# Turning the memory rows in two column parts and interleaving the Q and K passes by part in a recurrent attention layer

## The chip, the cores and the metric

The kernel runs on one core of one Trainium2 chip. The metric is the time of one launch on the device in microseconds (us). PE is the tensor engine, PEld its weight loads, DVE the vector engine, ACT the scalar engine, POOL (Pool) the general engine.

## The reference, cut to what matters

Four layers run on 2048 tokens of width 640: A, B, A, B. Only B is touched. It walks through 64 segments of 32 tokens, and each segment's first 8 rows are the memory that the segment before produced, so the steps cannot overlap freely:

```python
mem = mem0                                             # 8 memory rows
for s in range(n_seg):                                 # 64 steps, 32 tokens each
    h = jnp.concatenate([mem, xs], axis=1)             # 40 rows
    q, k, v = (einsum('btd,dhe->bhte', h, W) for W in (Wq, Wk, Wv))
    p = softmax(where(mask, einsum('bhqe,bhke->bhqk', q, k) * scale, -1e9))
    o = einsum('bhqk,bhke->bhqe', p, v)
    o = einsum('bhte,hed->btd', o, Wo)
    mem = o[:, :M, :]                                  # what the next step waits for
    outs.append(o[:, M:, :])
```

With two layers B there are 128 steps and 126 boundaries between steps.

## The kernel before

The width of 640 is held as NCH = 5 chunks of 128. `hT[s]` is the transposed input of step s; its columns 24:32 of each chunk are the memory rows. A pass (Q or K for one half of the heads) is five parts, one for each chunk, of four matmuls each. When a pass is complete, DVE transposes its result (`turn`) and casts the memory columns into `QT` or `KT`, which the scores read.

```python
def part(c):                                           # 4 matmuls, one for each column group of PE
    for j in range(4):
        nc.tensor.matmul(ps[32*j:32*j+32, :], lhsT=cols(c), rhs=wsel(Wt, c, b, j),
                         start=(c == 0), stop=(c == NCH-1), tile_position=(0, 32*j), ...)

class QKPass:
    def run(self, k=NCH):
        while k > 0 and self.parts:
            self.parts.pop(0)(); k -= 1
        if not self.parts:
            tq = turn(self.ps[:])                                         # DVE transpose, b_TQ
            place("dve", tq, self.b, heads(self.dst[s]), 0, 8, 24)        # DVE cast, memory columns
            if not last:
                place("pool", tq, self.b, heads(self.dst[s + 1]), 8, 32, 0)
# ... one step:
qk(W.wq, "b_Qa", 0, QT)
qk(W.wk, "b_Ka", 0, KT)
qk(W.wq, "b_Qb", 1, QT)
K1 = QKPass(W.wk, "b_Kb", 1, KT)
K1.run(2)
scores(0)             # mask matmuls, then matmuls whose weights are KT: first reader of b_KT
K1.run(3)
# ...
if i4 == 0 and T + 1 < NT:
    tail_cols(T + 1)  # Pool: the tail rows' copy b_hx, used a step later
V0 = VPass(0); V0.run(1); sums(0); normalise(0); V0.run(4)
# ... scores(1), V1, values(0), sums(1), normalise(1), values(1), filler pieces in between ...
op.run(8)             # last part of the output projection b_OPS
TM = wk.tile([128, 10, 32], F32, name="b_TM", tag="TM")
nc.vector.transpose(out=TM[:].rearrange("p g t -> p (g t)"), in_=ops[:])
for hf in range(2):
    nc.vector.tensor_tensor(out=hT[s + 1][64*hf:64*hf+64, :, 24:32], in0=TM[0:64, hf:10:2, 24:32],
                            in1=TM[64:128, hf:10:2, 24:32], op=ALU.add)
fill(9)               # the rest of the filler: tail passes (b_tail) or a deferred projection (b_OPSd)
```

The filler is work that no step waits for, put where PE would be idle. Steps come in fours (i4 = 0 to 3). Step 0 has b_OPSd as filler, steps 1, 2 and 3 have the V, Q and K passes of the next tile's tail rows (b_tail; called V, Q and K tails below). PSUM is the memory that PE writes its results to; the results of the passes, the scores and the fillers rotate through three slots.

## Time and profile before

| | before |
|---|---|
| median of the first 3 runs | 2334.03 us (2330.82 to 2334.85) |
| span of the profiled run | 2335.8 us |
| a step of layer B | 12.9 to 13.5 us |

The page of the profile, its busy times and the first line of its chain of what ended last:

```profile
PE 2225.5 (95%) x54988; PEld 1238.1 (53%) x54988; DVE 1576.3 (67%) x3618; ACT 950.3 (41%) x2207; POOL 1036.7 (44%) x2475
...
PE 80%; DVE 10%; ACT 5%; issue 2%; DMA 2%; POOL 0%; SPq 0%; DVEq 0%; ACTq 0%; POOLq 0%
```

PE is the bound, and DVE is 10% of the chain. The groups by form (busy us, mean ns of one, then idle time before them) give the costs of the operations in question:

```profile
L85 DVE STREAM_TRANSPOSE b_TM<-b_OPS 128x320 f32<-128x320 f32 x126 | 65.1, 517 | 118.2 <-PE b_OPS L85 118.2
...
L85 DVE TENSOR_TENSOR b_hT<-b_TM 64x40 bf16<-64x40 f32 x252 | 56.1, 223 | 8.6
```

The table of waits (total us, times, longest us):

```profile
PEld L85 <- DVE b_hT L85: 66.6, 126, 1.7
...
PEld L85 <- DVE b_KT L85: 16.0, 100, 0.2
```

A timeline of one step boundary, behind Q tails and into a step with i4 = 3. The columns are start us, duration us, engine, line, operation, output<-inputs, shapes, count, and in brackets the idle time before it with its releaser:

```profile
781.95 1.25 PE L85 MATMUL b_tail<-b_wq,b_hx 128*32 128x512 bf16 x20
...
782.18 0.52 DVE L85 STREAM_TRANSPOSE b_TM<-b_OPS 128x320 f32<-128x320 f32 x1 [0.44 <-PE b_OPS L85]
...
782.73 0.54 DVE L85 TENSOR_TENSOR b_hT<-b_TM 64x40 bf16<-64x40 f32 x2
...
783.32 3.36 PEld L85 LDWEIGHTS <-b_hT 128*32 128x32 bf16 x68 [0.61 <-DVE b_hT L85]
783.32 1.26 PE L85 MATMUL b_Qa<-b_wq,b_hT 128*32 128x512 bf16 x20
...
784.71 0.72 DVE L85 STREAM_TRANSPOSE b_TQ<-b_Qa 128x512 f32<-128x512 f32 x1 [0.69 <-POOL b_QTt L85]
785.46 0.23 DVE L85 CAST b_QT<-b_TQ 128x128 bf16<-128x128 f32 x1
...
785.79 0.72 DVE L85 STREAM_TRANSPOSE b_TQ<-b_Ka 128x512 f32<-128x512 f32 x1
786.54 0.23 DVE L85 CAST b_KT<-b_TQ 128x128 bf16<-128x128 f32 x1
...
787.00 0.24 PE L85 MATMUL b_SP<-c_mask,c_identb 128*32 128x160 bf16 x4
787.00 0.11 PEld L85 LDWEIGHTS <-b_KT 128*32 128x32 bf16 x4
...
787.30 0.41 PE L85 MATMUL b_Kb<-b_wk,b_hT 128*32 128x512 bf16 x4
```

The 20 filler matmuls start at 781.95. Matmuls of this form follow each other 54 ns apart when nothing is in the way (b_Qa to b_Ka in the same step: 20 in 1.09 us), so the filler covers 1.08 us and ends its issue at 783.03. DVE needs until 783.27 for the memory rows, and b_Qa starts at 783.32: PE lost 0.29 us. I call the start of b_Qa less the end of the filler's issue the boundary gap, and read it at all 126 boundaries. Its mean is 0.28 us behind K tails, 0.18 behind V tails, 0.29 behind Q tails, 0.04 behind b_OPSd (30 boundaries each), 1.28 at four boundaries without filler, and about 1.3 at each layer's first.

The lower half of the extract is the path that the change puts at risk: b_KT is finished 3.45 us after the start of b_Qa (786.77 - 783.32), and its first reader is a weight load at 3.68 us.

### The profile page before, as it was taken

Reading aid. Unit: us, or ns where it says so; the run is one execution under the profiler, and the core shown is the slowest. Engines: PE = TensorE matmul, PEld = TensorE weight load, DVE = VectorE, ACT = ScalarE, POOL = GpSimd, SP = SyncE. Lnnn points to the kernel's source line nnn. Section 1 sums busy time; section 2 is a strip of 40 time slices with the busy share of each in tenths; the row PEclk is TensorE's granted clock in tenths of the full one; section 3 lists DMA queues with packets and bytes.
Section 4 is the critical chain, followed back from the end, with each engine's and each line's share of the span. In section 5 each row is a group of like instructions: output and inputs, shape, how many; then the busy total and the mean of one; then the engine's idle time right before and its main releaser. Section 6 shows DMA issues by size and latency. Waiting matters only on the chain.

```text
span 2335.8 us, 122651 instructions
## 1 busy us (share of the span) xinstructions
PE 2225.5 (95%) x54988; PEld 1238.1 (53%) x54988; DVE 1576.3 (67%) x3618; ACT 950.3 (41%) x2207; POOL 1036.7 (44%) x2475
## 2 busy tenths in 40 slices
PE   6999989999999999999889899899999999999997
PEld 3444545555555555555545445455555555555554
DVE  5777746666666666666657777566666666666664
ACT  5776823323232333323257767223333233323332
POOL 3344534444444444444324445344444444444442
PEclk9999989999999999999989999999999999999998
DMA  6555540000000000000133334300000000000000
GB/s 165 146 148 152 161 142 20 21 18 20 18 19 19 20 21 20 21 15 17 31 104 115 108 117 127 124 18 15 17 15 17 16 18 16 17 18 16 14 12 14
DMA packets 90649, 123.38 MB, mean 53 GB/s; under 512 B 16496, under 2 KB 80000, under 8 KB 88192
## 3 DMA queue, kind: packets, MB, share of 16 engines
q1 hardware_dynamic: 87648, 111.84, 16.9%
q8 instruction: 431, 7.06, 1.3%
q10 hardware_dynamic: 2464, 3.61, 0.6%
q14 instruction: 106, 0.87, 0.1%
HBM read 89.17 MB, written 26.21 MB: 49 GB/s over the span
## 4 chain that ended last, share of the span: by engine, by line
PE 80%; DVE 10%; ACT 5%; issue 2%; DMA 2%; POOL 0%; SPq 0%; DVEq 0%; ACTq 0%; POOLq 0%
PE b_OPS L85 14%; PE b_V L85 13%; PE b_Qa L85 7%; PE b_tail L85 7%; PE b_Kb L85 6%; PE b_Ka L85 6%; PE b_Qb L85 6%; PE b_SP L85 4%; PE a_PP L85 4%; ACT a_PT L85 4%; PE b_OTL L85 3%; PE b_OPSd L85 3%; PE a_S L85 2%; PE a_pv L85 2%; DVE a_qk L85 2%
## 5 line engine op out<-in xcount | busy, mean ns | idle before, releaser
L85 PEld LDWEIGHTS <-b_hT 128*32 128x32 bf16 x15120 | 369.8, 96 | 334.7 <-DVE b_hT L85 66.6
L85 ACT ACTIVATE b_PT<-b_SP 128x224 bf16<-128x224 f32 x256 | 92.2, 360 | 784.6 <-DVE b_TQ L85 740.2
L85 PE MATMUL b_V<-b_wv,b_hT 128*32 128x512 bf16 x5040 | 355.8, 381 | 0.0
L85 ACT ACTIVATE a_PT<-a_S 128x768 bf16<-128x768 f32 (+1 forms) x384 | 326.7, 892 | 62.4 <-PE a_S L85 56.2
L85 PE MATMUL b_OPS<-b_wo,b_OTsb 128*32 128x320 bf16 x8192 | 329.9, 303 | 6.5 <-DVE b_OTsb L85 5.2
L85 PEld LDWEIGHTS <-b_OTsb 128*32 128x32 bf16 x8192 | 197.3, 97 | 115.4 <-DVE b_OTsb L85 49.4
L85 POOL CAST b_QT<-b_TQ 128x384 bf16<-128x384 f32 x254 | 142.7, 562 | 240.9 <-DVE b_TQ L85 240.9
L85 ACT CAST b_OTsb<-b_OTL 128x320 bf16<-128x320 f32 x384 | 151.0, 428 | 232.3 <-PE b_OTL L85 204.7
L85 POOL CAST b_KT<-b_TQ 128x384 bf16<-128x384 f32 x254 | 142.9, 563 | 175.5 <-DVE b_TQ L85 174.3
L85 POOL TENSOR_TENSOR b_PT<-b_PT,b_R 128x64 bf16<-128x64 bf16 x256 | 105.6, 412 | 222.1 <-ACT b_R L85 197.4
L85 POOL TENSOR_SCALAR_AFFINE_SELECT a_PT<-a_PT 128x256 bf16<-128x256 bf16 x256 | 109.0, 427 | 172.6 <-ACT a_PT L85 161.0
L85 PE MATMUL b_Kb<-b_wk,b_hT 128*32 128x512 bf16 x2520 | 182.5, 380 | 0.0
L85 PE MATMUL b_Qa<-b_wq,b_hT 128*32 128x512 bf16 x2520 | 162.3, 387 | 13.7 <-DVE b_hT L85 7.2
L85 PE MATMUL b_Ka<-b_wk,b_hT 128*32 128x512 bf16 x2520 | 160.0, 383 | 0.0
L85 PE MATMUL b_Qb<-b_wq,b_hT 128*32 128x512 bf16 x2520 | 158.1, 380 | 0.0
L85 PE MATMUL a_PP<-a_xnT,a_wt 128*128 128x512 bf16 x560 | 146.1, 394 | 5.2 <-DVE a_um L85 1.5
L85 DVE STREAM_TRANSPOSE b_TM<-b_OPS 128x320 f32<-128x320 f32 x126 | 65.1, 517 | 118.2 <-PE b_OPS L85 118.2
L85 PE MATMUL a_S<-a_qk 32*128 32x512 bf16 (+3 forms) x1024 | 137.3, 308 | 7.8 <-ACT a_PT L85 6.5
L85 DVE CAST b_Vsb<-b_V 128x512 bf16<-128x512 f32 x128 | 88.5, 692 | 74.6 <-PE b_SP L85 43.9
L85 DVE TENSOR_TENSOR b_PT<-b_PT,b_R 128x160 bf16<-128x160 bf16 x256 | 103.8, 405 | 48.3 <-ACT b_R L85 29.2
L85 DVE STREAM_TRANSPOSE b_TQ<-b_Qa 128x512 f32<-128x512 f32 x128 | 91.7, 717 | 65.7 <-PE b_Qa L85 45.4
L85 DVE CAST b_OTsb<-b_OTL 128x320 bf16<-128x320 f32 x128 | 62.9, 492 | 106.0 <-PE b_OTL L85 105.2
(165 smaller groups left out, 4270.0 us busy)
## 6 DMA issues: line engine op xcount, KB each, us to landing
a_wt<-a_wpad SPq DMA_DIRECT2D x112, 160.0 KB
b_XO<-xres SPq DMA_DIRECT2D x256, 30.0 KB
a_wvo<-in_A_wo_dram SPq DMA_DIRECT2D x8, 800.0 KB
b_wq<-in_B_Wq_dram SPq DMA_DIRECT2D x20, 256.0 KB
b_wk<-in_B_Wk_dram SPq DMA_DIRECT2D x20, 256.0 KB
xres<-a_xo SPq DMA_DIRECT2D x16, 320.0 KB
xres_bf<-a_xb SPq DMA_DIRECT2D x32, 160.0 KB
b_wv<-in_B_Wv_dram SPq DMA_DIRECT2D x20, 256.0 KB
```

Of the source, the lines that this page charges most:

```text
L85: r = f(*a, **k)
```

## The change

The intent is to let PE begin the next step on chunks 0 and 1 while DVE still turns the other three, and to have enough matmuls on those two chunks (Q and K, 16 of them) to bridge the rest. The tail rows' copy on Pool moves from before the first scaling to behind the second. The whole diff:

```diff
-            qk(W.wq, "b_Qa", 0, QT)
-            qk(W.wk, "b_Ka", 0, KT)
+            Q0, K0 = QKPass(W.wq, "b_Qa", 0, QT), QKPass(W.wk, "b_Ka", 0, KT)
+            Q0.run(2)
+            K0.run(2)
+            Q0.run(3)
+            K0.run(3)
             qk(W.wq, "b_Qb", 1, QT)
@@
             while xn_pending:
                 ln_tr(xn_pending.pop(0))
-            if i4 == 0 and T + 1 < NT:
-                tail_cols(T + 1)
             V0 = VPass(0)
@@
             normalise(1)
+            if i4 == 0 and T + 1 < NT:
+                tail_cols(T + 1)
             if g_need < NT:
@@
                 TM = wk.tile([128, 10, 32], F32, name="b_TM", tag="TM")
-                nc.vector.transpose(out=TM[:].rearrange("p g t -> p (g t)"), in_=ops[:])
-                for hf in range(2):
-                    nc.vector.tensor_tensor(out=hT[s + 1][64 * hf:64 * hf + 64, :, 24:32], in0=TM[0:64, hf:10:2, 24:32],
-                                            in1=TM[64:128, hf:10:2, 24:32], op=ALU.add)
+                for c0, c1 in ((0, 2), (2, NCH)):
+                    nc.vector.transpose(out=TM[:, 2 * c0:2 * c1].rearrange("p g t -> p (g t)"), in_=ops[:, 64 * c0:64 * c1])
+                    for hf in range(2):
+                        nc.vector.tensor_tensor(out=hT[s + 1][64 * hf:64 * hf + 64, c0:c1, 24:32], in0=TM[0:64, 2 * c0 + hf:2 * c1:2, 24:32],
+                                                in1=TM[64:128, 2 * c0 + hf:2 * c1:2, 24:32], op=ALU.add)
```

## The prediction

> **What bounds the kernel.** PE is busy 95% of the span and holds 80% of the chain that ended last (the page). Layer B is 128 recurrent steps of about 13.0 us. At each boundary (timelines of PE) the last 32 b_OPS matmuls are covered by 20 tail matmuls (54 ns apart, 1.08 us) or 36 b_OPSd matmuls (1.22 us). Meanwhile DVE runs one 128x320 transpose (517 ns) and two 64x40 adds (about 200 ns each, 310 to 370 ns where Pool's b_OTdef copy overlaps); b_Qa needs all of it, 1.16 us after b_OPS. By b_Qa's start less the filler's issue time, PE loses 0.28 us entering a step behind K tails (30 boundaries), 0.29 us behind Q tails (30), 0.18 us behind V tails (30), 0.04 us behind b_OPSd (30), and 1.28 us at the four boundaries with no filler. That is 33 us in all.
>
> **What the change does.**
> 1. First part: 128 columns. From 717 ns for 512 and 517 ns for 320 columns, a transpose is about 184 ns + 1.04 ns a column: 317 ns for 128, 384 ns for 192. So chunks 0 and 1 are ready about 0.25 us earlier. DVE gains three instructions a step, about 0.55 us. The Trainium skill ("Perfetto Trace Analysis", section Optimizing Scalar/DVE Operations) says that breaking up instructions may let work finish sooner where an unsaturated engine makes bubbles elsewhere; the trace has that bubble, 0.28 us.
> 2. The second part comes some 0.85 us after the first. Q and K on chunks 0 and 1 are 16 matmuls, 0.87 us: just enough.
> 3. Gain: 30 x 0.25 + 30 x 0.26 + 30 x 0.15 + 6 x 0.25 = about 21 us.
> 4. Cost: the interleaving finishes b_Qa after 28 matmuls instead of 20, 0.43 us later. Today Qa's transpose starts 1.39 us after the first Qa matmul and K's 128x128 cast into b_KT ends at 3.45 us; the first scores need b_KT at 3.68 us. After: Qa's transpose at 1.82, then 0.72 + 0.23 + 0.72 + 0.23 us and three gaps of 0.03, back to back on DVE, ending at about 3.81, seen by PE at 3.86. So a new stall of 0.11 to 0.18 us opens before the first scores in every step: 126 x 0.11 to 0.18 = 14 to 23 us given back.
> 5. The tail rows' copy (407 ns on Pool, 30 times) precedes Pool's first scaling, which ended at 1013.71 in the step I read; values began at 1013.84 without waiting. Moving it saves nothing.
>
> **Prediction.** Net gain of some 5 us: 2328 us, range 2314 to 2341. Faster by over 2%: 0.03; within 2%: 0.95; slower by over 2%: 0.02.
>
> **What would show it.** b_TM in two forms, near 317 and 384 ns. The b_Qa boundary gap near 0.03 us behind tails, and waits of PE or its weight loads on b_hT sharply lower. In the table of waits, weight loads waiting for b_KT rising from 16 us (the second scores only) to 30 us or more. DVE busy up by about 65 us. Steps behind OPSd (second of four) longer, the others shorter or equal.
>
> **What would make it wrong.** If Qa's transpose starts sooner than 1.82, or b_KT is needed later, the stall vanishes and the gain is near 20 us (2314). If part 2 is late (Pool's copies blocking the adds), a second gap in mid-Q appears and the kernel is a few us slower.

## The result, and the profile after

The changed kernel took 2314.97 us (median of 4 runs, 2309.22 to 2318.51) against 2333.35 us for the kernel before on the same chip. The ratio is 0.992, 95% interval 0.9898 to 0.9942. A ratio here and below is the mean time of one kernel's fast runs over that of the other's of the same rounds, so it is not quite the ratio of the medians. A second set of runs gave 2316.59 us and 0.9923. The forecast of 2328 us had the sign right and the range (2314 to 2341) held the result at its edge, but the gain, 17 to 18 us by the medians (14 to 24 by the interval), is more than three times the forecast 5 us.

The page, busy times:

```profile
PE 2209.5 (96%) x54988; PEld 1232.1 (53%) x54988; DVE 1622.9 (70%) x3996; ACT 950.0 (41%) x2207; POOL 1030.1 (45%) x2475
```

The groups by form:

```profile
L85 DVE TENSOR_TENSOR b_hT<-b_TM 64x24 bf16<-64x24 f32 x252 | 50.3, 200 | 8.7
L85 DVE TENSOR_TENSOR b_hT<-b_TM 64x16 bf16<-64x16 f32 x252 | 49.6, 197 | 8.6
L85 DVE STREAM_TRANSPOSE b_TM<-b_OPS 128x192 f32<-128x192 f32 x126 | 48.2, 383 | 3.9
...
L85 DVE STREAM_TRANSPOSE b_TM<-b_OPS 128x128 f32<-128x128 f32 x126 | 40.0, 317 | 118.7 <-PE b_OPS L85 118.7
```

The table of waits:

```profile
PEld L85 <- DVE b_hT L85: 69.5, 219, 1.4
...
PEld L85 <- DVE b_KT L85: 35.6, 222, 0.2
```

The timeline of the same boundary:

```profile
775.05 1.25 PE L85 MATMUL b_tail<-b_wq,b_hx 128*32 128x512 bf16 x20
775.27 0.32 DVE L85 STREAM_TRANSPOSE b_TM<-b_OPS 128x128 f32<-128x128 f32 x1 [0.44 <-PE b_OPS L85]
...
775.63 0.48 DVE L85 TENSOR_TENSOR b_hT<-b_TM 64x16 bf16<-64x16 f32 x2
775.68 0.40 POOL L85 COPY b_OTdef<-b_OTsb 128x256 bf16<-128x256 bf16 x1
776.13 0.38 DVE L85 STREAM_TRANSPOSE b_TM<-b_OPS 128x192 f32<-128x192 f32 x1
...
776.16 0.61 PE L85 MATMUL b_Qa<-b_wq,b_hT 128*32 128x512 bf16 x8
776.55 0.39 DVE L85 TENSOR_TENSOR b_hT<-b_TM 64x24 bf16<-64x24 f32 x2
776.60 0.60 PE L85 MATMUL b_Ka<-b_wk,b_hT 128*32 128x512 bf16 x8
...
777.00 2.52 PEld L85 LDWEIGHTS <-b_hT 128*32 128x32 bf16 x52 [0.29 <-DVE b_hT L85]
777.03 0.82 PE L85 MATMUL b_Qa<-b_wq,b_hT 128*32 128x512 bf16 x12
...
777.98 0.72 DVE L85 STREAM_TRANSPOSE b_TQ<-b_Qa 128x512 f32<-128x512 f32 x1 [0.28 <-PE b_Qa L85]
...
778.73 0.23 DVE L85 CAST b_QT<-b_TQ 128x128 bf16<-128x128 f32 x1
...
778.87 0.71 DVE L85 STREAM_TRANSPOSE b_TQ<-b_Ka 128x512 f32<-128x512 f32 x1
...
779.61 0.23 DVE L85 CAST b_KT<-b_TQ 128x128 bf16<-128x128 f32 x1
...
779.84 0.24 PE L85 MATMUL b_SP<-c_mask,c_identb 128*32 128x160 bf16 x4
779.89 0.10 PEld L85 LDWEIGHTS <-b_KT 128*32 128x32 bf16 x4 [0.16 <-DVE b_KT L85]
...
780.13 0.41 PE L85 MATMUL b_Kb<-b_wk,b_hT 128*32 128x512 bf16 x4
```

The filler's issue ends at 776.13 and b_Qa starts at 776.16: the gap is 0.03 us. The 16 matmuls of the first part last until 777.03, and the second part reaches PE at 777.00: just enough. So far this is the forecast. The surprise is below. Counted from the start of b_Qa, b_KT is finished at 3.68 us (I had 3.81), the weight load that needs it runs at 3.73, and b_Kb resumes at 3.97, where it resumed at 3.98 before. The load "waited 0.16 us", and PE lost nothing, because the mask matmuls were still running. The medians over all 128 steps agree with this one: b_KT is finished at 3.67 to 3.69 us and b_Kb resumes at 3.96 to 3.97, except in the steps with i4 = 0 (3.75 and 4.03); before the change b_Kb resumed at 3.97 in all four.

Boundary gaps and step times tell where all of it came from. A gap is a mean over its boundaries; a step runs from one b_Qa to the next, so it includes the gap at its end (medians of the first layer B).

| us | gap: K tails | b_OPSd | V tails | Q tails | no filler (4) | step i4=0 | 1 | 2 | 3 |
|---|---|---|---|---|---|---|---|---|---|
| before | 0.28 | 0.04 | 0.18 | 0.29 | 1.28 | 12.94 | 12.96 | 13.06 | 13.48 |
| after | 0.03 | 0.00 | 0.00 | 0.04 | 1.03 | 12.94 | 12.77 | 12.80 | 13.23 |

The gaps fall from 31 us to 8 us in sum, by 23 us. Four steps shrink by 0.70 us together, and 32 times that is 22.4 us; by these medians only about 1 us of the 23 is given back, all in the steps with i4 = 0. Summed over every step of both layers, from b_Qa to b_Qa, the time falls by 20.6 us, so it may be 2 us. The two profiled spans differ by 22.4 us, more than the medians of the runs do, in part because the profiled run of the kernel before (2337.55 us) was 3 to 7 us slower than the timed ones.

### The profile page after: what moved, and what is told of

Its sections match the earlier page's. It is cut to its first block, busy times and chain, and to the rows that moved or that the text cites. A ratio compares the mean times of both kernels' runs of the same rounds, so it can differ in the third digit from the quotient of the medians.

```text
span 2313.4 us, 123029 instructions
## 1 busy us (share of the span) xinstructions
PE 2209.5 (96%) x54988; PEld 1232.1 (53%) x54988; DVE 1622.9 (70%) x3996; ACT 950.0 (41%) x2207; POOL 1030.1 (45%) x2475
## 4 chain that ended last, share of the span: by engine, by line
PE 81%; DVE 8%; ACT 5%; issue 3%; DMA 2%; SPq 1%; POOL 0%; DVEq 0%; ACTq 0%; POOLq 0%
PE b_OPS L85 13%; PE b_V L85 12%; PE b_tail L85 9%; PE b_Kb L85 6%; PE b_Qa L85 6%; PE b_Ka L85 6%; PE b_Qb L85 6%; PE b_SP L85 5%; ACT a_PT L85 4%; PE a_PP L85 4%; PE b_OTL L85 3%; PE b_OPSd L85 3%; PE a_S L85 2%; PE a_pv L85 2%; DVE a_qk L85 2%
## 5 line engine op out<-in xcount | busy, mean ns | idle before, releaser
L85 PEld LDWEIGHTS <-b_hT 128*32 128x32 bf16 x15120 | 370.4, 96 | 310.5 <-DVE b_hT L85 69.5
L85 PE MATMUL b_Qa<-b_wq,b_hT 128*32 128x512 bf16 x2520 | 182.5, 384 | 5.0 <-DVE b_hT L85 5.0
L85 PE MATMUL b_Ka<-b_wk,b_hT 128*32 128x512 bf16 x2520 | 181.4, 382 | 0.0
L85 DVE STREAM_TRANSPOSE b_TM<-b_OPS 128x128 f32<-128x128 f32 x252 | 88.2, 350 | 122.7 <-PE b_OPS L85 118.7
L85 POOL TENSOR_TENSOR b_Rtot<-b_Rtot,b_R 128x160 bf16<-128x160 bf16 x256 | 127.0, 496 | 0.0
```

The costliest lines, as they stand in the source:

```text
L85: r = f(*a, **k)
```

## The experiments

All kernels gave correct results. Runs of the first group (the changed kernel again and the first three below) shared one chip and its runs of the kernel before (median 2333.59 us); the last four shared another (2336.32 us).

| kernel | median us | ratio to before | 95% interval |
|---|---|---|---|
| the change again | 2316.59 | 0.9923 | 0.9906 to 0.9941 |
| split only | 2358.11 | 1.0105 | 1.0088 to 1.0122 |
| interleaving only | 2337.77 | 1.0010 | 0.9993 to 1.0028 |
| copy moved back | 2315.83 | 0.9921 | 0.9903 to 0.9938 |
| one more cast | 2360.80 | 1.0102 | 1.0085 to 1.0118 |
| three more casts | 2429.63 | 1.0400 | 1.0386 to 1.0415 |
| cut at 3 | 2351.52 | 1.0071 | 1.0055 to 1.0087 |
| cut at 1 | 2362.69 | 1.0121 | 1.0102 to 1.0139 |

The change once more, for comparison in the same rounds:

> The changed kernel once more, timed in the same rounds as the three below. Both theories: 0.990 to 0.994 of the time before, near 2315 us.

It came out as expected.

**1. The split alone.** The change without its first hunk and without the moved copy (the two hunks of the copy are left out here):

```diff
-            Q0, K0 = QKPass(W.wq, "b_Qa", 0, QT), QKPass(W.wk, "b_Ka", 0, KT)
-            Q0.run(2)
-            K0.run(2)
-            Q0.run(3)
-            K0.run(3)
+            qk(W.wq, "b_Qa", 0, QT)
+            qk(W.wk, "b_Ka", 0, KT)
```

> Only the memory rows' turn in two parts; Q and K passes in their old order, the copy in its old place. Theory (the split needs the interleaving: the second part lands about 0.80 us after the start of b_Qa as in the changed kernel's trace, while b_Qa alone wants chunk 2 after 8 matmuls, 0.43 us): a hole of about 0.35 us inside b_Qa in every step, against a boundary gap smaller by 0.25, 0.18, 0.25 and 0.04 us; net 30 x (0.10 + 0.17 + 0.10 + 0.31) = about 20 us slower than before, near 2354 us, ratio about 1.009. Rival (the early first part alone earns the gain, the interleaving is ornament): near 2315 us, ratio 0.992.

Measured: 2358.11 us, ratio 1.0105, slower than before by 24.5 us. The rival falls. The gaps at the boundary are those of the changed kernel (0.03, 0.00, 0.00, 0.04), but the timeline of the same step shows the hole that takes their place:

```profile
787.45 0.61 PE L85 MATMUL b_Qa<-b_wq,b_hT 128*32 128x512 bf16 x8
787.85 0.39 DVE L85 TENSOR_TENSOR b_hT<-b_TM 64x24 bf16<-64x24 f32 x2
...
788.29 2.93 PEld L85 LDWEIGHTS <-b_hT 128*32 128x32 bf16 x60 [0.72 <-DVE b_hT L85]
788.29 0.83 PE L85 MATMUL b_Qa<-b_wq,b_hT 128*32 128x512 bf16 x12 [0.23 <-DVE b_hT L85]
```

Eight matmuls take 0.43 us, and the ninth starts 0.84 us after the first: a hole of 0.41 us. Splitting delays the last chunk (two transposes and four adds instead of one and two), so without work to bridge it, it is a loss.

**2. The interleaving alone.** The first hunk alone, the turn in one piece, the copy in its old place.

```diff
-            qk(W.wq, "b_Qa", 0, QT)
-            qk(W.wk, "b_Ka", 0, KT)
+            Q0, K0 = QKPass(W.wq, "b_Qa", 0, QT), QKPass(W.wk, "b_Ka", 0, KT)
+            Q0.run(2)
+            K0.run(2)
+            Q0.run(3)
+            K0.run(3)
```

> Only the interleaving of the Q and K passes; the turn in one piece. My prediction's term (b_Qa's later end makes b_KT late, 0.11 to 0.18 us stall in each step): 14 to 23 us slower than before, 2348 to 2357 us. The theory formed from the trace of the changed kernel (DVE catches up: the transpose of b_Ka starts 0.14 us after the start of the cast before it, where I had 0.26, and b_KT arrives just as the mask matmuls end): within 0.2% of before, 2330 to 2338 us, with boundary gaps as before (0.28, 0.18, 0.29, 0.04 us).

Measured: 2337.77 us, ratio 1.0010 (0.9993 to 1.0028), with the gaps and step medians of the kernel before to within 0.01 us. The interval excludes my forecast's 14 us (a ratio of 1.006). The timeline shows the same late b_KT as in the changed kernel, without loss:

```profile
784.97 0.23 DVE L85 CAST b_KT<-b_TQ 128x128 bf16<-128x128 f32 x1
...
785.20 0.24 PE L85 MATMUL b_SP<-c_mask,c_identb 128*32 128x160 bf16 x4
785.25 0.10 PEld L85 LDWEIGHTS <-b_KT 128*32 128x32 bf16 x4 [0.16 <-DVE b_KT L85]
...
785.49 0.84 PE L85 MATMUL b_Kb<-b_wk,b_hT 128*32 128x512 bf16 x12
```

b_Qa started at 781.52 here, so b_Kb resumes 3.97 us later, as in the other two kernels. In the table of waits, weight loads waiting for b_KT rose to 35.4 us as I had forecast, and that wait is worth nothing.

**3. The copy back in its old place.** The changed kernel without its second and third hunks.

```diff
+            if i4 == 0 and T + 1 < NT:
+                tail_cols(T + 1)
             V0 = VPass(0)
@@
             normalise(1)
-            if i4 == 0 and T + 1 < NT:
-                tail_cols(T + 1)
```

> The changed kernel with the tail rows' copy on Pool back in its old place. Theory (that copy is off the critical path): the same as the changed kernel, within 3 us. Rival (the unpredicted part of the gain, some 13 us, comes from the moved copy: 30 copies of 0.41 us): 8 to 13 us slower than the changed kernel.

Measured: 2315.83 us against 2316.59 us for the changed kernel in the same rounds. The moved copy earns nothing that these runs can see.

**4. One and three more casts.** The next two runs ask how near the edge b_KT is now. The DVE cast of Qa's memory columns is made two or four times, writing the same values (`range(1)` in the first, `range(3)` in the second).

```diff
                         tq = turn(self.ps[:])
                         place("dve", tq, self.b, heads(self.dst[s]), 0, 8, 24)
+                        if self.b == 0 and self.dst is QT:
+                            for _ in range(1):
+                                place("dve", tq, self.b, heads(self.dst[s]), 0, 8, 24)
```

> The changed kernel with the DVE cast of Qa's rows into b_QT made twice (the second writes the same values), so that b_KT comes one DVE instruction later. Theory (in the changed kernel b_KT reaches PE just when the mask matmuls before the first scores end, with no slack, so my stall was real in kind but its size is zero): all of the added DVE time, 0.13 to 0.26 us, shows as a stall in each of 128 steps: 17 to 33 us slower than the changed kernel, 2332 to 2349 us. Rival (b_KT still has slack of 0.2 us or more): unchanged at 2315 us.

> The same with three added casts. Theory: three times the effect of one added cast, 51 to 100 us slower than the changed kernel, 2366 to 2415 us; the ratio of the two effects near 3 says that there is no slack, a ratio well over 3 says how much there was. Rival (slack of 0.2 us): the effect is three casts less 0.2 us a step.

Measured: 2360.80 and 2429.63 us, some 44 and 113 us above the changed kernel (across the two chips; the kernel before differs by 3 us between them). The rival of 0.2 us of slack falls. Both figures missed my ranges (2332 to 2349 and 2366 to 2415 us), because the first added cast costs more than the 0.13 to 0.26 us that I put in. The timeline with one added cast, the same step:

```profile
791.21 0.67 DVE L85 CAST b_QT<-b_TQ 128x128 bf16<-128x128 f32 x2
791.27 0.53 POOL L85 CAST b_QT<-b_TQ 128x384 bf16<-128x384 f32 x1
791.80 0.70 DVE L85 STREAM_TRANSPOSE b_TQ<-b_Ka 128x512 f32<-128x512 f32 x1
...
792.54 0.23 DVE L85 CAST b_KT<-b_TQ 128x128 bf16<-128x128 f32 x1
...
792.82 0.10 PEld L85 LDWEIGHTS <-b_KT 128*32 128x32 bf16 x4 [0.16 <-DVE b_KT L85]
...
793.04 0.84 PE L85 MATMUL b_Kb<-b_wk,b_hT 128*32 128x512 bf16 x12
```

Two casts span 0.67 us; a single one takes 0.23. The second runs beside Pool's cast and ends only after it (it took 0.41 us; with three added casts, the last two, behind Pool's cast, took 0.23 us each). The Trainium skill ("SBUF — State Buffer", section Who interferes with whom) says that a DVE instruction with two inputs in SBUF (the memory that holds the kernel's other tiles) contends with a Pool instruction that reads SBUF, that one in a two-port mode, which a cast can enter, contends with Pool too, and that the one issued first has the shared ports for the whole instruction. The trace agrees in kind; which mode the casts ran in, no run shows. b_Qa started at 788.64, so b_KT's load is at 4.18 us instead of 3.73, 0.45 later, and b_Kb resumes at 4.40 instead of 3.97, 0.43 later: practically all of the delay is paid. With three added casts the load is at 4.70 us, 0.97 later. The step medians grew by 0.44, 0.43 and 0.42 us for i4 = 1, 2 and 3 with one cast, and by 0.97, 0.95 and 0.95 us with three, so in these steps nothing but a few hundredths of a microsecond is forgiven; steps with i4 = 0 grew by 0.27 and 0.98 us. The ratio of the two costs, 2.6, says less than I had hoped, since the casts do not cost the same. The listed wait of the load is 0.16 us in all these kernels, whatever PE lost. One thing I had not foreseen: here the mask matmuls move too, because their PSUM slot is the one that b_Ka's transpose frees, so they hide nothing.

**5. Other cuts.** The same change with the cut behind chunk 3, and behind chunk 1 (passes 1, 1, 4, 4):

```diff
-            Q0.run(2)
-            K0.run(2)
             Q0.run(3)
             K0.run(3)
+            Q0.run(2)
+            K0.run(2)
@@
-                for c0, c1 in ((0, 2), (2, NCH)):
+                for c0, c1 in ((0, 3), (3, NCH)):
```

> The changed kernel with the cut behind chunk 3 instead of 2: parts of 192 and 128 columns, Q and K passes run 3, 3, 2, 2. Theory: the first part is ready 0.08 us later (about 5 us in all), and b_Qa ends after 32 matmuls instead of 28, 0.22 us later, which with no slack makes b_KT late by 0.22 us in every step, 28 us: together some 34 us slower than the changed kernel, near 2349 us, ratio to before about 1.007. Rival (b_KT has slack, only the boundary counts): near 2320 us, ratio 0.994.

> The changed kernel with the cut behind chunk 1: parts of 64 and 256 columns, passes run 1, 1, 4, 4. Theory: the first part comes 0.09 us earlier, of little use since the filler already covers it; the second part comes about 0.9 us after the first while only 8 matmuls, 0.43 us, stand in between: a hole of 0.28 to 0.38 us in the passes in every step, about 38 us slower than the changed kernel, near 2353 us, ratio about 1.008. Rival (the earlier the first part the better): 2312 us or less.

Cut at 3: 2351.52 us where I expected 2349. The sum came out right partly by luck: the gaps cost 13 us more than in the changed kernel where I had counted 5, and the later b_KT cost less than my 28 us (by the sum of all steps 24 us, since the steps with i4 = 0 grew by only 0.15 us). The gaps are 0.25 behind K tails, 0.23 behind Q tails, 0.01 behind V tails, where I had counted 0.08 us more than in the changed kernel. In the same step of its trace, the first add started 0.01 us after a Pool copy of 0.40 us, and the two adds took 0.64 us instead of 0.39. The stall before the first scores is there: b_KT's load at 3.95 us after b_Qa's start and b_Kb at 4.18, 0.21 us later than in the changed kernel. Cut at 1: 2362.69 us, about 10 us slower than expected; the second part reached PE 0.92 us after the start of b_Qa, with 8 matmuls (0.43 us) to cover it. Both rivals fall. The cut at 2 is the only one of the three that satisfies both ends: a second part bridged by the first one's matmuls, and a b_Qa that ends early enough.

No experiment pointed to a kernel faster than the changed one: 8 us of gaps are left, 6 of them at the six boundaries that have no filler, and there is no slack at b_KT to trade.

## Why the prediction was right or wrong

- **The bound and the gain at the boundary: right.** Forecast 21 us from shorter gaps, measured 23 us. The two transposes were forecast at 317 and 384 ns and took 317 and 383. The Trainium skill ("Perfetto Trace Analysis", section Optimizing Scalar/DVE Operations) on breaking up instructions agrees with this trace, with the condition that experiment 1 adds: the later part needs work to cover it, or the split costs 24.5 us.
- **The second part "just enough": right**, by 0.03 us in the step shown (777.00 against 777.03).
- **The moved copy "saves nothing": right** (2315.83 against 2316.59 us).
- **The failed step: point 4, "a new stall of 0.11 to 0.18 us opens before the first scores in every step ... 14 to 23 us given back".** Experiment 2 measures the interleaving at a ratio of 1.0010 (0.9993 to 1.0028), and the changed kernel's steps give back 1 to 2 us. The mechanism is real: one more DVE cast there costs 44 us, and of the 35 us that a cut at 3 costs, some 22 to 24 are not boundary gaps. The mis-sized term is the DVE chain from b_Qa's transpose to b_KT, "0.72 + 0.23 + 0.72 + 0.23 us and three gaps of 0.03". It measured 1.86 us (777.98 to 779.84), where I had 1.99. The first and third gaps were about 0.03 us. The middle one was -0.09: b_Ka's transpose starts at 778.87 while the cast before it ends at 778.96. Transpose to cast is a dependent pair and kept its gap in all 128 steps; cast to the next transpose is an independent pair, and their recorded spans overlapped in 126 of 128. Independence alone is not the condition: the two adds into b_hT, neither of which reads what the other writes, stood 0.03 us apart at all 126 boundaries, and so did the second part's transpose behind the first part's adds. What decides it was not tested. The 0.13 us took the stall from 0.11 to nothing.
- **That the range held was luck.** The prediction named this outcome ("the stall vanishes and the gain is near 20 us (2314)"), and 2314.97 us lies 1 us inside the range whose lower end is this number. But neither cause that it gave came true: b_Qa's transpose started at 1.82 us, as forecast, and the mask matmuls before the first scores at 3.68, as before. What was shorter was the chain between them.
- **That was visible before.** In the trace before the change, DVE mostly stood 0.10 us idle between cast and transpose, but where it did not, the very pairs in question overlapped by up to 0.09 us (b_QT's cast and b_Ka's transpose in 3 of 128 steps, b_KT's cast and b_Qb's transpose in 4). In the timeline of DVE another independent pair overlaps by 0.08 us:

```profile
1012.72 0.54 DVE L85 TENSOR_TENSOR b_PT<-b_PT,b_R 128x160 bf16<-128x160 bf16 x1
1013.18 1.00 DVE L85 TENSOR_TENSOR b_XO<-b_OPS,b_XO 64x320 f32<-64x320 f32 x2
```

  The skill's same section gives an overhead of each DVE instruction as time that the engine is busy, and says that the profiled latency is about twice this, "since the write-acknowledgement half overlaps with the next instruction". These traces agree for cast and transpose, by 0.08 to 0.09 us, but not for the two adds into b_hT. I cited that section and still added up spans.
- **The signs I named: half of them misled.** Weight loads waiting for b_KT rose from 16.0 to 35.6 us, as forecast, at no cost. Their waits on b_hT did not fall (66.6 to 69.5 us) although the gaps lost 23 us. The Trainium skill ("TensorE: Matmul & The Clock Gate", section Architectural detail) says that PE can pull weight loads ahead of matmuls in flight; these traces agree in that the loads' waits lie partly or wholly under running matmuls, 0.32 of the 0.61 us at the boundary shown before, and all of the 0.16 us at b_KT after. The boundary gap and the step time were the right measures.
- **"Steps behind OPSd longer": wrong.** They fell from 12.96 to 12.77 us. The steps that gained nothing are those with i4 = 0. In the one read, DVE's cast into b_QT took 0.30 us beside two Pool copies, b_KT's load came 3.80 us after b_Qa and b_Kb resumed at 4.02 us, 0.05 late, which eats the 0.04 us gained at the end. That the Pool copies are the cause was not tested separately.
- **DVE busy:** forecast +65 us, measured +46.6 us on the page. The new instructions cost what I had counted: the groups by form above add up to 188.1 us instead of 121.2, 66.9 more. The page counts a moment once, and the overlapping part of DVE's spans grew from 50 to 71 us.

## What to carry to other kernels

Splitting an operation on the critical path pays only with enough independent work on the first part to cover the second, and with the reader of the interleaved work still on time; check both ends, since the three cuts tried here spread over 46 us. When you add up a chain of instructions on one engine from a trace, take start-to-start distances of the same pair of operations, at a place where nothing else holds the second, not spans plus gaps: 0.12 us in one gap turned a forecast loss of 14 us or more into nothing. Judge PE's losses from the spacing of its matmuls, not from the table of weight-load waits.

## What the Trainium skill lacked or had wrong

- "Perfetto Trace Analysis", section Optimizing Scalar/DVE Operations: it states the overlap with the next instruction but not, in that section, for which pairs. Here dependent DVE neighbours stood 0.03 us apart, and independent ones overlapped by 0.08 to 0.09 us of recorded span (cast and transpose) or stood 0.03 us apart as well (the two adds into b_hT). What the skill says elsewhere about when a DVE instruction is held was not tested here.
- "VectorE: DVE Perf Modes", section The three transpose paths: for DVE that section has one figure, 311 ns for 128x128 bf16, and none for other sizes. Here f32 transposes from PSUM on 128 partitions took 250, 317, 383, 450, 517 and 717 ns for 64, 128, 192, 256, 320 and 512 columns: about 183 ns plus 1.04 ns a column (fitted to these six).
- No page says that a wait charged to a weight load is not time lost on PE: in experiment 2 these waits on b_KT rose from 16.0 to 35.4 us beside a ratio of 1.0010.
